# Two groups' value products of batch 0 moved ahead of the first up product, with dummy matmuls behind them

## The chip, the core and the metric

One core of a Trainium2 chip runs the whole program. The metric is the device time of one launch in microseconds (us); below 0.2% of it, a difference can hardly be told from none. Six runs of the kernel before gave 334.09, 333.66, 332.86, 333.53, 332.96 and 333.91 us, median 333.6 us.

## What is computed

The reference is an attention with projected keys and values (8 batches, 8 heads, 1024 positions, head size 64, projected length 64), followed by a two-matrix maximum and an output product:

```python
k_proj = np.einsum('ks,bhsd->bhkd', E, k)
v_proj = np.einsum('ks,bhsd->bhkd', F, v)
scores = scale * np.matmul(q, k_proj.transpose(0, 1, 3, 2))
attn = softmax(scores)                      # over the 64 projected positions
x = attn @ v_proj                           # heads side by side: 8192 x 512
out = np.maximum(x @ w1, x @ w2) @ w_out    # 512 -> 1024 -> 512
```

The kernel takes max(h1, h2) as h2 + relu(h1 - h2): it multiplies x by the weight difference wd = w1 - w2 (the "up product"), applies relu, multiplies by w_out, and adds x @ M with M = w2 @ w_out. Sums are kept in fp32, operands in fp16.

## The kernel before

**Stages.** Each batch goes through an attention part (projections, scores, exponentials, column sums, products with v) and an up and a down part. Batches are cut in two halves of 512 rows (`o` or `j` = 0, 1). From batch 1 on, the up and down parts use a 2x2 block scheme with seven products per unit, whose pieces are interleaved by a list of slots with the attention steps of a later batch. Batch 0 is different: its eight up products per half (`up_slots`, L394) are plain, and beside them the weights are still being prepared: four differences of 256 columns each (`step_wd`, L413, on VectorE), transposes of w2 (`step_w2t`, L419), and the four products that make M (`step_m`, L433, each copied out of PSUM by ScalarE at L440).

**Attention of batch 0.** It is written out by hand in L713 to L747. A group is (g, j): g picks four of the eight heads, j one half of the rows. For each of the four groups there are scores with an exponential on ScalarE (`step_sc`), sums with a logarithm (`step_dn`), the inverse as a second exponential (`step_inv`), and the products with v (`step_at`, L318): 16 small matmuls (`values_into`, L288, tiles of 64x32 with 256 columns, L278) and two multiplications by the inverse sums on VectorE (L325), which write x into `xt_sb`. Half j of x is whole when groups (0, j) and (1, j) have been multiplied; the up product of half j (L400) contracts over four row blocks r, of which r = 0, 1 come from g = 0 and r = 2, 3 from g = 1.

**PSUM banks.** Four banks mm0 to mm3 are handed out in turn by `mm_bank()` (L60, list `turn`, L58); a tile named `att_ps` has two banks and two buffers (`att_banks`, L66). A bank is given to its next writer when its last reader is done. With the last of the products that make M, the slot list reaches key (0, 19): L812 sets `turn` to [2, 3], so that the next bank handed out is mm2, and `step_kv` for batch 1 (its projections of k and v, L172, matmuls at L180) takes it. The first down products, which follow it, name their banks, mm0 and mm1.

**Order.** Every engine runs its instructions in the order in which they are written, under a manual schedule: the order of the list is the order of the queue, and waits are put in by data and buffers. After L747 the slots of L762 follow: the up product 0 of half 0, the value products of group (0, 1), the up product 1 of half 0, those of group (1, 1), the second weight difference, then the up products of half 1 and so on. `warm(n)` (L137) issues n matmuls of 128x512 on a tile of ones, whose result is not used.

**Loads.** k, q, v and the weights come in through GpSimd's DMA queue (L102, L126, L130), in the order of the calls, one after another; the pool for k, v and q has four buffers. Stores and DMA transposes go through SyncE's queue.

```python
    step_at(t, 1, 0)
    step_wd(0)
    ...
    slots = [
        (0, u0[0]), (None, f(step_at, 0, 1)), (1, u0[1]), (None, f(step_at, 1, 1)),
        (None, lambda: loads(1, "v", "q", "k")),
        (None, wd[1]), (2, u1[0]), (3, u1[1]), (4, u0[2]), (None, wt[0]), (5, u0[3]),
```

Of the kernel before, what the change touches and what calls it, by code (L numbers as in the profile page):

```python
# [16 lines left out]
def kernel(  # L17
# [42 lines left out]
    def mm_bank(dtype=FP32, n=None):  # L60
        if n is None:
            n = turn.pop(0)
            turn.append(n)
        return ps.tile([128, 512 if dtype == FP32 else 1024], dtype, tag=f"mm{n}", name="mm_ps")

    def att_banks(dtype=FP32):  # L66
        return ps.tile(
            [128, 2, 512 if dtype == FP32 else 1024], dtype, tag="att", bufs=2, name="att_ps"
        )
# [27 lines left out]
    def load_all(t, b, n, src):  # L97
        alloc(t, n)
        load(t, n, src, b, 0, H)
# [37 lines left out]
    def warm(n):  # L137
        w_ps = mm_bank()
        for _ in range(n):
            nc.tensor.matmul(  # L140
                out=w_ps, lhsT=ones16[:, 0:128], rhs=ones16, start=True, stop=True
            )
# [145 lines left out]
    def values_into(t, g, j, at_ps):  # L288
        for z in range(2):
            tiles_into(  # L290
                lambda o: at_ps[o][:, z * W : (z + 1) * W], t["ex", g, j],
                lambda rows, hh: t["vp"][rows, 4 * g + hh, z, :],
            )

    def new_xt(t):
        t["xt"] = xpool.tile([128, NP2, 2, HALF], FP16, tag="xt", name="xt_sb")

    def x_out(t, g, j):
        return t["xt"][:, 2 * g : 2 * g + 2, :, j * W : (j + 1) * W]
# [15 lines left out]
        ld = t["ld", g, j]  # L315
        nc.scalar.activation(out=ld, in_=ld, func=ACTF.Exp, scale=-1.0)

    def step_at(t, g, j):  # L318
        if "xt" not in t:
            new_xt(t)  # L320
        ld = t.pop(("ld", g, j))
        at_ps = [mm_bank() for _ in range(2)]
        values_into(t, g, j, at_ps)
        for o in range(2):
            nc.vector.tensor_tensor(  # L325
                out=x_out(t, g, j)[:, :, o, :],
                in0=at_ps[o].rearrange("q (z n) -> q z n", z=2),
                in1=ld[:, o, None, :].broadcast_to([128, 2, W]),
                op=ALU.mult,
            )  # L330
# [63 lines left out]
    def up_slots(t, j):  # L394
        t["gt", j] = gt = gpool.tile([128, NFB, HALF], FP16, tag="gt", name="gt_sb")
        for fb in range(NFB):
            def up(fb=fb):
                h_ps = mm_bank()
                for r in range(NDC):
                    nc.tensor.matmul(  # L400
                        out=h_ps,
                        lhsT=wd_sb[:, r, fb * 128 : (fb + 1) * 128],
                        rhs=t["xt"][:, r, :, j * W : (j + 1) * W],
                        start=(r == 0), stop=(r == NDC - 1),
                    )
                if fb < 3:
                    nc.scalar.activation(out=gt[:, fb, :], in_=h_ps, func=ACTF.Relu)
                else:
                    nc.vector.tensor_scalar_max(gt[:, fb, :], h_ps, 0.0)
            yield up  # L410


    def step_wd(f0):  # L413
        nc.vector.tensor_tensor(  # L414
            out=wd_sb[:, :, f0 : f0 + 256], in0=w1_sb[:, :, f0 : f0 + 256],
            in1=w2_sb[:, :, f0 : f0 + 256], op=ALU.subtract,
        )

    def step_w2t(f0):  # L419
        ps_t = mm_bank(FP16)  # L420
        for f in range(2):
            for r in range(NDC):
                nc.tensor.transpose(
                    out=ps_t[:, (f * NDC + r) * 128 : (f * NDC + r + 1) * 128],
                    in_=w2_sb[:, r, f0 + f * 128 : f0 + (f + 1) * 128],
                    identity=ident16,
                )
        fb = f0 // 128
        nc.scalar.copy(
            out=w2t_sb[:, fb : fb + 2, :].rearrange("q f m -> q (f m)"), in_=ps_t  # L430
        )
# [281 lines left out]
    t = tiles[0]  # L713
# [25 lines left out]
    step_dn(t, 1, 0)  # L739
    step_inv(t, 1, 0)  # L740
    step_at(t, 0, 0)
    step_dn(t, 1, 1)
    step_inv(t, 0, 1)
    step_kv(t, 4, 8, "v")
    step_inv(t, 1, 1)
    step_at(t, 1, 0)
    step_wd(0)  # L747


    load_all(tiles[1], 1, "k", k)  # L750
    u0, u1 = [*up_slots(t, 0)], [*up_slots(t, 1)]
    wt = [lambda f0=f0: step_w2t(f0) for f0 in range(0, DF, 256)]
    wd = [lambda f0=f0: step_wd(f0) for f0 in range(0, DF, 256)]
    f = lambda s, *a: lambda: s(tiles[0], *a)

    def loads(b, *names):
        for n in names:
            b_ = b + (n == "k" and b < 2)
            if b_ < B:
                load_all(tiles[b_], b_, n, {"k": k, "v": v, "q": q}[n])  # L760

    slots = [  # L762
        (0, u0[0]), (None, f(step_at, 0, 1)), (1, u0[1]), (None, f(step_at, 1, 1)),
        (None, lambda: loads(1, "v", "q", "k")),
        (None, wd[1]), (2, u1[0]), (3, u1[1]), (4, u0[2]), (None, wt[0]), (5, u0[3]),
        (None, wd[2]), (None, wt[1]), (6, u1[2]), (7, u1[3]), (8, u0[4]), (9, u0[5]), (None, wd[3]),
        (None, wt[2]), (10, u1[4]), (11, u1[5]), (12, u0[6]), (13, u0[7]), (None, wt[3]),
        (14, u1[6]), (15, u1[7]),
# [41 lines left out]
    t = tiles[1]  # L810
    at_slot((0, 19), new_attn, t)
    at_slot((0, 19), lambda: turn.__setitem__(slice(None), [2, 3]))  # L812
    for n, x in enumerate((
# [4 lines left out]
        for name in x.split():  # L818
# [6 lines left out]
            else:  # L825
                g, j = int(name[2]), int(name[3])
# [9 lines left out]
    t = tiles[2]  # L836
# [8 lines left out]
    for b in range(3, B):  # L845
        t = tiles[b]
# [75 lines left out]
```

The softmax here doesn't subtract the row's maximum and nothing guards it: scores larger than these inputs give would overflow.

## Time and profile before

| what | value |
|---|---|
| median of six runs | 333.6 us |
| the profiled execution, its own time | 334.09 us |
| its span (first to last instruction) | 332.3 us |
| TensorE matmul busy | 319.6 us (96%) |
| VectorE busy / ScalarE busy | 239.8 us (72%) / 201.5 us (61%) |
| mean granted TensorE clock | 0.995 |

The profiled execution is also the longest of the six runs. PE is TensorE's matmul, PEld its weight load, DVE is VectorE, ACT ScalarE, POOL GpSimd and SP SyncE. A row of the timeline gives the start, the length, the engine, the line, the operation with its output and inputs, and in brackets how long the engine had been idle and what ended that. A row of the windows gives the length of a stretch, the busy time of each engine in it with the number of instructions in brackets, the granted clock of TensorE as a share of full speed, the DMA share and GB/s. The chain is the work that ended last, followed back step by step; its rows give the start, the length and the work.

### The profile page before, as it was taken

The page shows a single profiled execution, that of the slowest core. Times are in us where ns is not written, and L with a number is a line of the kernel's source. Part 1 is how long each engine was busy: PE and PEld are TensorE (multiplying, and loading weights), DVE is VectorE, ACT ScalarE, POOL GpSimd, SP SyncE. Part 2 cuts the span into 40 slices and gives each one's busy share as a digit, 9 for nine tenths or more (in the row PEclk, how much of TensorE's full clock was granted, in tenths as well). Part 3 has the DMA queues.
Part 4 walks back from the last instruction along what each step waited for, and adds up shares of the span by engine and source line. Part 5 has one row for each costly group of instructions (what it writes and reads, how often), then busy time and mean ns, then how long its engine had stood idle before and what let it go on. Part 6 is the DMA issues. An engine that isn't in the chain of part 4 may idle for free.

```text
span 332.3 us, 9012 instructions
## 1 busy us (share of the span) xinstructions
PE 319.6 (96%) x3852; PEld 247.8 (75%) x3852; DVE 239.8 (72%) x426; ACT 201.5 (61%) x358; POOL 37.1 (11%) x56
## 2 busy tenths in 40 slices
PE   8967999999999999999999999998999999999994
PEld 3532546658888788878887788877887888888883
DVE  1354698988676779677969777776967796969572
ACT  2462522754677677767777677766776777764541
POOL 8546002003000030003000210003000000000000
PEclk9997999999999999999999999999999999999999
DMA  8999999998994969994999699894999321212132
GB/s 150 202 199 197 207 207 192 204 195 150 199 240 126 185 93 224 196 221 85 199 238 200 112 161 242 200 179 67 218 221 190 86 96 34 97 34 95 35 127 96
DMA packets 74681, 53.14 MB, mean 160 GB/s; under 512 B 29457, under 2 KB 74513, under 8 KB 74641
## 3 DMA queue, kind: packets, MB, share of 16 engines
q0 software_dynamic: 29376, 28.31, 53.8%
q1 hardware_dynamic: 45264, 24.25, 30.6%
q8 instruction: 30, 0.49, 0.6%
q14 instruction: 11, 0.08, 0.1%
HBM read 57.15 MB, written 16.78 MB: 222 GB/s over the span
## 4 chain that ended last, share of the span: by engine, by line
PE 85%; DMA 7%; DVE 4%; issue 1%; POOL 1%; ACT 0%; DVEq 0%; SPq 0%; POOLq 0%
PE mm_ps L632 42%; PE mm_ps L554 25%; PE mm_ps L400 4%; PE att_ps L180 3%; DMA big<-in_moe_w_dram 3%; PE mm_ps L266 3%; PE att_ps L278 3%; DMA k_sb<-in_k_dram 2%; PE mm_ps L436 2%; DMA kpt_sb<-kp_sb 1%; DVE xt_sb L325 1%; DVE o_sb L656 1%; PE mm_ps L278 1%; POOL k_sb L102 1%; DVE gt_sb L569 1%
## 5 line engine op out<-in xcount | busy, mean ns | idle before, releaser
L525 ACT COPY p_sb<-mm_ps 128x512 f32<-128x512 f32 x172 | 97.2, 593 | 46.8 <-PE mm_ps L554 33.2
L632 PEld LDWEIGHTS <-big 128*128 128x128 f16 x768 | 73.4, 98 | 12.3 <-issue 3.7
L632 PE MATMUL mm_ps<-T_sb,big 128*128 128x256 f16 x576 | 78.1, 273 | 0.0
L569 DVE TENSOR_TENSOR gt_sb<-mm_ps,p_sb 128x512 f16<-128x512 f32 x56 | 38.5, 688 | 47.6 <-PE mm_ps L554 47.5
L554 PE MATMUL mm_ps<-big,big 128*128 128x256 f16 x336 | 50.4, 273 | 0.0
L554 PEld LDWEIGHTS <-big 128*128 128x128 f16 x448 | 43.8, 98 | 5.2
L632 PEld LDWEIGHTS <-gt_sb 128*128 128x128 f16 x384 | 35.6, 98 | 10.1 <-issue 5.8
L632 PE MATMUL mm_ps<-wo_sb,gt_sb 128*128 128x256 f16 x256 | 42.9, 274 | 0.1
L554 PEld LDWEIGHTS <-wd_sb 128*128 128x128 f16 x336 | 32.9, 98 | 4.1 <-issue 0.3
L554 PE MATMUL mm_ps<-xt_sb,wd_sb 128*128 128x256 f16 x224 | 33.6, 273 | 0.2 <-ACT ex_sb L351 0.2
L351 ACT ACTIVATE ex_sb<-mm_ps 128x512 f16<-128x512 f32 x48 | 26.1, 596 | 10.2 <-PE att_ps L278 7.0
L656 DVE TENSOR_TENSOR o_sb<-mm_ps,p_sb 128x512 f32<-128x512 f32 x32 | 21.9, 684 | 10.7 <-PE mm_ps L632 7.2
L377 DVE TENSOR_TENSOR xt_sb<-att_ps,ld_sb 128x1024 f16<-128x1024 f32 x24 | 29.2, 1218 | 0.1
L632 PE MATMUL mm_ps<-m_sb,xt_sb 128*128 128x256 f16 x128 | 24.4, 273 | 0.0
L604 ACT ACTIVATE gt_sb<-mm_ps 128x512 f16<-128x512 f32 x28 | 16.8, 600 | 8.7 <-PE mm_ps L554 8.7
L515 DVE TENSOR_TENSOR big<-gt_sb 128x1024 f16<-128x1024 f16 x32 | 21.9, 684 | 0.2
L572 DVE TENSOR_SCALAR gt_sb<-gt_sb 128x512 f16<-128x512 f16 (+1 forms) x56 | 20.3, 362 | 1.9
L632 PE MATMUL mm_ps<-wo_sb,big 128*128 128x256 f16 x128 | 21.5, 273 | 0.0
L632 PE MATMUL mm_ps<-T_sb,gt_sb 128*128 128x256 f16 x128 | 21.5, 273 | 0.0
L632 PEld LDWEIGHTS <-xt_sb 128*128 128x128 f16 x192 | 18.8, 98 | 2.2
L229 POOL COPY junk<-kpt_sb 1x1 f16<-1x1 f16 x5 | 0.9, 178 | 167.4 <-DMA kpt_sb<-kp_sb 167.4
L400 PE MATMUL mm_ps<-xt_sb,wd_sb 128*128 128x512 f16 x64 | 16.3, 400 | 3.0 <-DVE wd_sb L414 2.1
(86 smaller groups left out, 434.7 us busy)
## 6 DMA issues: line engine op xcount, KB each, us to landing
out_dram<-o_sb SPq DMA_DIRECT2D x63, 256.0 KB, 2.7
k_sb<-in_k_dram POOLq DMA_DIRECT2D x7, 1024.0 KB, 10.2
v_sb<-in_v_dram POOLq DMA_DIRECT2D x7, 1024.0 KB, 17.2
q_sb<-in_q_dram POOLq DMA_DIRECT2D x7, 1024.0 KB, 22.2
k_sb<-in_k_dram POOLq DMA_DIRECT2D x4, 256.0 KB, 6.6
q_sb<-in_q_dram POOLq DMA_DIRECT2D x4, 256.0 KB, 7.7
v_sb<-in_v_dram POOLq DMA_DIRECT2D x2, 512.0 KB, 12.5
big<-in_moe_w_dram POOLq DMA_DIRECT2D x8, 128.0 KB, 10.6
```

Source lines behind the costliest of these rows:

```text
L278: nc.tensor.matmul(out=dst(r ^ (hh % 2))[hh * Z : (hh + 1) * Z, :], lhsT=weights(rows, hh), rhs=ex[rows, hh % 2, hh // 2 * W : (hh // 2 + ...
L351: nc.scalar.activation(out=t["ex", g, j][:, e, :], in_=banks[e], func=ACTF.Exp, scale=scale)
L377: nc.vector.tensor_tensor(out=x_out(t, g, j).rearrange("q z o n -> q o z n"), in0=at_ps.rearrange("q o (z n) -> q o z n", z=2), in1=ld[:, ...
L400: nc.tensor.matmul(out=h_ps, lhsT=wd_sb[:, r, fb * 128 : (fb + 1) * 128], rhs=t["xt"][:, r, :, j * W : (j + 1) * W], start=(r == 0), stop= ...
L515: nc.vector.tensor_tensor(out=S(i), in0=x, in1=y, op=op)
L525: copy(out=x, in_=bank)
L554: nc.tensor.matmul(out=bank[:, m * W : (m + 1) * W], lhsT=w_[:, n_, (2 * d + m) * 128 : (2 * d + m + 1) * 128], rhs=a[:, n_, :], start=(n ...
L569: nc.vector.tensor_tensor(out=c_blk(j, c), in0=two(x), in1=two(y), op=ALU.add)
L572: nc.vector.tensor_scalar_max(ap, ap, 0.0)
L604: nc.scalar.activation(out=out, in_=in_, func=ACTF.Relu)
L632: nc.tensor.matmul(out=bank[:, i * CH : (i + 1) * CH], lhsT=a(c)[:, i * 128 : (i + 1) * 128], rhs=w_(c), start=(n is not None and m == (lo ...
L656: nc.vector.tensor_tensor(out=o_sb, in0=two(x), in1=two(y), op=ALU.add)
```

## The change

Both remaining value products of batch 0, of groups (0, 1) and (1, 1), are written directly behind `step_wd(0)`, ahead of the first up product, and leave the slot list. They take the two-bank tiles of `att_banks` in place of two banks of the turn each. Four dummy matmuls follow them. The first weight difference, which had stood ahead of the slots already, stands on VectorE ahead of the multiplications of these two groups. In the slot list the loads of the next tiles and the second weight difference change their places relative to the up products of half 1. No instruction of VectorE, ScalarE, GpSimd or SyncE changes its place among those of its own engine: on VectorE the order was already the multiplications of group (1, 0), the first weight difference, those of groups (0, 1) and (1, 1), the second difference. The four multiplications read another PSUM tile. TensorE has the 32 small matmuls at another place and four matmuls with their weight loads more. Between the value products and the end of the preparation `mm_bank()` is called three times less (four banks less for the two groups, one more for the dummies), so that every later bank of the turn in batch 0 is another one than before, up to the reset of `turn` at key (0, 19).

```diff
-    def step_at(t, g, j):
+    def step_at(t, g, j, att=False):
         if "xt" not in t:
             new_xt(t)
         ld = t.pop(("ld", g, j))
-        at_ps = [mm_bank() for _ in range(2)]
+        if att:
+            both = att_banks()
+            at_ps = [both[:, o, :] for o in range(2)]
+        else:
+            at_ps = [mm_bank() for _ in range(2)]
         values_into(t, g, j, at_ps)
...
     step_at(t, 1, 0)
     step_wd(0)
+    step_at(t, 0, 1, True)
+    step_at(t, 1, 1, True)
+    warm(4)
...
     slots = [
-        (0, u0[0]), (None, f(step_at, 0, 1)), (1, u0[1]), (None, f(step_at, 1, 1)),
-        (None, lambda: loads(1, "v", "q", "k")),
-        (None, wd[1]), (2, u1[0]), (3, u1[1]), (4, u0[2]), (None, wt[0]), (5, u0[3]),
+        (0, u0[0]), (1, u0[1]), (None, lambda: loads(1, "v", "q", "k")), (2, u1[0]), (3, u1[1]),
+        (None, wd[1]), (4, u0[2]), (None, wt[0]), (5, u0[3]),
```

## The prediction

> **What bounds the kernel now.** The page first: matmuls fill 319.6 of 332.3 us, and the chain of work that ended last is 85% TensorE. What TensorE loses, the program loses. The row of the 40 slices shows a granted clock below full only in slices 0 and 3; slice 3 (24.9 to 33.2 us) holds the change. So next I read the chain of waits over 20 to 32 us:
>
> ```profile
> 24.58 0.68 DVE xt_sb L325
> 25.25 0.61 DVE wd_sb L414
> 25.86 0.04 issue
> 25.91 1.89 PE mm_ps L400 x4
> 27.80 0.56 PE mm_ps L278 x15
> 28.35 1.25 PE mm_ps L400 x4
> 29.60 0.39 PE mm_ps L278 x16
> ...
> 30.70 0.69 DVE xt_sb L325
> ...
> 31.43 0.59 PE mm_ps L400 x2
> ```
>
> VectorE, TensorE and VectorE take turns here. The value products of groups (0, 1) and (1, 1) (L278 at 27.80 and 29.60) stand behind up products, so their multiplications (L325) end only at 31.38, and the first up product of half 1 goes on at 31.43 with r = 2, 3. The timeline shows who was idle meanwhile:
>
> ```profile
> 23.96 1.29 DVE L325 TENSOR_TENSOR xt_sb<-mm_ps,ld_sb 128x512 f16<-128x512 f32 x2 [0.61 <-ACT ld_sb L316]
> 25.17 0.68 DVE L414 TENSOR_TENSOR wd_sb<-big,big 128x1024 f16<-128x1024 f16 x1
> 25.91 1.89 PE L400 MATMUL mm_ps<-xt_sb,wd_sb 128*128 128x512 f16 x4 [2.09 <-DVE wd_sb L414]
> 28.50 1.29 DVE L325 TENSOR_TENSOR xt_sb<-mm_ps,ld_sb 128x512 f16<-128x512 f32 x2 [2.65 <-ACT gt_sb L407]
> 30.09 1.29 DVE L325 TENSOR_TENSOR xt_sb<-mm_ps,ld_sb 128x512 f16<-128x512 f32 x2 [0.30 <-PE mm_ps L278]
> ```
>
> TensorE waits 2.09 us for the first weight difference; VectorE then has nothing to do for 2.65 us. And 1.89 us for four matmuls is 0.43 us each at first, where 0.216 is the full-speed pitch (16 in 3.45 us at 35.50). The windows say why: the clock is halved for one stretch of 3.41 us, after one in which TensorE was busy for 1.22 us.
>
> ```profile
> 18.67:22.08 3.41, 2.35 (x70) 1.41 (x56) 1.05 (x3) 2.94 (x4) 0.73 (x2) 1.00 1.34 199
> 22.08:25.49 3.41, 1.22 (x32) 0.68 (x26) 2.61 (x6) 1.63 (x3) 3.41 (x5) 1.00 1.44 195
> 25.49:28.90 3.41, 2.99 (x22) 0.86 (x23) 0.76 (x2) 0.60 (x1) 3.41 (x5) 0.50 1.27 203
> ```
>
> **The moved products.** Group (1, 0)'s products start at 23.41. The 32 small matmuls follow at 0.34 to 0.39 us for 16 (chain, 29.60), so they end at about 24.5. Their inputs are there: the two `att_ps` buffers are free after the logarithms (L312), which end at 21.27 and 23.44, and the last inverse ends at 24.47. All of it lies in the 2.09 us wait and costs nothing.
>
> **VectorE.** Its order does not change: the first difference at 25.17 keeps its place, so the first up product still starts at 25.91. The multiplications now follow it directly. A 128x1024 fp16 difference lets the next one start 0.60 us after it (49.00, 49.60, 50.20), and a pair of multiplications takes 1.21 to the next start (23.96 to 25.17). So (0, 1) starts at 25.77 and (1, 1) at 26.98, not 30.09: 3.11 us earlier. It ends at 28.27, and the up product of half 1 goes on at 28.32. The new tile for these reads is costed at nothing: the nearest row, L377 on `att_ps`, does both halves at once in 1218 ns, against 1.29 for the pair; the bounds are -0.15 and +0.1 us in all.
>
> **The dummies.** Four take 4 x 0.216 = 0.87 us, 24.5 to 25.4, inside the wait; without that cover they would cost 0.87. They lift the busy time of the window ending at 25.49 from 1.22 to about 2.7 us (0.7 from the products' move, 0.8 from the dummies) of 3.41, above the 2.35 that kept the full clock. Then eight up matmuls take 1.73 us, 25.91 to 27.64, and r = 0, 1 end at 28.07: TensorE idles 0.25 us, and VectorE sets the 28.32. The Trainium skill speaks otherwise: TensorE: Matmul & The Clock Gate, section "Why this matters for your kernels", asks only that no idle gap exceed about 3 us. By it a gap of 2.09 would not have lowered the clock, and filling it would not be what brings it back; the halved clock would stay, 0.43 us each until 28.9, and r = 2, 3 would start at about 29.55: 1.88 us earlier, not 3.11. I take the row: 1.22 of 3.41 busy, and the clock fell as that stretch ended.
>
> **The shifted banks.** Counted from the top, the dummies take mm2, which before was the first up product's. Behind them come 16 up products, 4 transposes and 4 products of M, 24 calls in all, so that the last of these (L436) is in mm2 again; before, four more calls (the groups') stood among them, the first up product was the first of 28, and the last was in mm1. The projections of batch 1 (L180), next on TensorE, ask for mm2, because the turn is reset there. Before, mm2 held the first product of M, long copied, and mm1's next writer came over 1.85 us later. The edge, before:
>
> ```profile
> 51.87 0.40 PE L180 MATMUL mm_ps<-k_sb,eft 128*64 128x512 f16 x1
> ...
> 51.97 0.59 ACT L440 CAST m_sb<-mm_ps 128x512 f16<-128x512 f32 x1 [1.14 <-PE mm_ps L436]
> ```
>
> The projections must now wait for that copy: 51.97 + 0.59 + 0.04 for the release is 52.60, against 51.87: 0.73 us of bare TensorE idling (bounds 0.6 and 0.8). Queued behind it is every later matmul; the chain from 51.94 to 66.69 has no slack, so it is lost in full. ScalarE and VectorE idle there anyway (1.29 and 1.04 us before their next copies).
>
> **Fixed dates.** Loads do not move: GpSimd's order is unchanged, and up to the load issued at 54.08, which a projection releases, nothing on its queue waits for shifted work. Issue plus landing against the new need: last weights 24.92 + 7.7 = 32.6, where the third difference is due at 32.59 and its matmul 0.8 us behind the difference's end; w_out 37.7 against 41.5; v of batch 1 at 48.1 against 49.5; its q at 28.26 + 25.1 = 53.36, needed at 56.06 - 3.11 + 0.73 = 53.68. That one is close: 2.65 us earlier is the most it allows. q of batch 2 lands at 70.65 either way, and its transposes are in by 78.5 (GpSimd's gate), against scores at 82.56 - 2.38 = 80.2. The later loads are released by work that shifts too.
>
> **The sum.** 3.11 - 0.73 = 2.38 us: span 332.3 - 2.4 = 329.9, time 334.09 - 2.38 = 331.7. That execution was the longest of six. The halved clock depends on where the stretch of 3.41 us falls, which may differ by run: with full clock before, its first two up products and the products between would have ended 1.5 us sooner, near 332.6; the runs lie between. The changed kernel should miss that spread and lie near 331.7, 1.9 us (0.6%) under the median of 333.6.
>
> **Rivals.**
> - *The bank wait costs nothing* (the copy is hidden, or I counted the turn wrongly): then 3.11 is cut to 2.65 by q of batch 1: 331.4. Against it: the named banks and the contiguous chain. 0.14.
> - *The clock still falls at 25.5*, as small 64x32 matmuls and four dummies might not count enough: 1.88 - 0.73 = 1.15, 332.9. For it: the skill's rule, and that nothing in the trace shows the threshold between 36% and 69% busy. Against: the estimated 79%. 0.12.
> - *Slower: the clock stays halved through two stretches*, 25.5 to 32.3. Then TensorE, bound by its matmuls from 25.9 on, loses half of 6.4 us less the 0.25 slack, 2.95: 331.7 + 2.95 = 334.6. It decides only if the stretch from 25.49 is judged idle too; before, one that was 2.99 of 3.41 busy restored the clock. 0.03.
> - *A load is later than in this trace*: each 0.1 us of q of batch 1 past 53.7 costs 0.1; by 1 us, 332.4. Inside the range. 0.08.
>
> The likeliest, 331.7 within 0.4, has 0.63. The range, 331.0 to 332.9, takes in the bounds of the copy and the multiplications (0.3 together), the first rival, the late load, and the upper rival's time. Below 0.2% (0.67 us, about what a measurement of this kernel tells from no change), that is below 332.9, lie the main case, the first and last rival and part of the second: faster 0.88; same 0.08; slower 0.04.
>
> **What would show it.** The first up product's four matmuls at 25.9 in about 0.9 us, clock 1.00 in every stretch; multiplications of L329 at 25.8 and 27.0; the second up product of half 0 without products between; the first matmuls of L180 for batch 1 near 49.5 with a wait of about 0.7 us for ScalarE's copy (L444); no wait for q of batch 1. A clock of 0.50 after 25.5 means the second rival; no gap ahead of L180 the first. I am wrong if a wait that I called hidden appears between 28 and 70 us.

## The result, and the profile after

The changed kernel takes 331.29 us in the median of 18 runs (330.07 to 332.64), the kernel before 333.58 us in 39 runs taken beside it and earlier. The ratio is 0.9932, with a 95% interval of 0.9917 to 0.9947: 2.3 us faster (1.8 to 2.8). Forecast were 331.7 us: a difference of 2.38 us within one execution, and of 1.9 us against the median of 333.6.

The profiled execution has a span of 328.3 us, 4.0 less than the one of before, which is more than the 2.3 us by which the medians differ. To see what of it belongs to the change, I cut each profiled execution at three points that all kernels here have: the start of the first weight difference on VectorE, the end of the first 20 matmuls of the up products (five products, half 1 begun), and the first matmul of batch 1's projections (L180). What lies before the first point is the start-up, which no kernel here changes. (From L329 on, lines of the changed kernel stand four further down: its L404 is L400 of before.)

| kernel | start-up | to the 20th up matmul | to L180 of batch 1 | rest | span |
|---|---|---|---|---|---|
| before | 25.17 | 8.58 | 18.12 | 280.46 | 332.3 |
| changed | 24.48 | 5.45 | 18.86 | 279.51 | 328.3 |

The change is in the middle columns: 3.13 us less and 0.74 us more. The other 1.6 us are the start-up, 0.69, where v landed earlier, and the rest, 0.9, which has one place, shown further down. The prediction spoke of neither.

The slices of the page after have no dip in the clock any more:

```profile
PEclk9999999999999999999999999999999999999999
```

The timeline of the changed kernel around the first up product, the rows that answer to those of before:

```profile
22.95 0.62 PE L278 MATMUL att_ps<-ex_sb,vp_sb 64*32 64x256 f16 x32
23.28 1.29 DVE L329 TENSOR_TENSOR xt_sb<-mm_ps,ld_sb 128x512 f16<-128x512 f32 x2 [0.61 <-ACT ld_sb L316]
23.50 1.04 PE L140 MATMUL mm_ps<-ones 128*128 128x512 f16 x4
24.48 0.68 DVE L418 TENSOR_TENSOR wd_sb<-big,big 128x1024 f16<-128x1024 f16 x1
25.08 2.48 DVE L329 TENSOR_TENSOR xt_sb<-att_ps,ld_sb 128x512 f16<-128x512 f32 x4
25.22 4.71 PE L404 MATMUL mm_ps<-xt_sb,wd_sb 128*128 128x512 f16 x20 [0.68 <-DVE wd_sb L418]
```

Both value products (32 small matmuls) and the dummies fit into the wait, of which 0.68 us is left; the four multiplications follow the weight difference without a gap; and 20 up matmuls run in one row of 4.71 us. The chain shows who sets the pace now, VectorE with a bare 0.04 us between:

```profile
26.36 1.21 DVE xt_sb L329 x2
27.57 0.04 issue
27.61 2.32 PE mm_ps L404 x10
```

The windows, at the same times as before (busy times in the order PE, PEld, DVE, ACT, POOL, then clock, DMA share, GB/s), have the full clock in both:

```profile
22.08:25.49 3.41, 2.21 (x58) 1.03 (x55) 2.64 (x5) 1.63 (x3) 3.41 (x6) 1.00 1.43 195
25.49:28.90 3.41, 3.35 (x16) 1.42 (x15) 2.67 (x5) 1.79 (x3) 3.38 (x5) 1.00 1.24 199
```

And the chain at the end of M's products has the new wait:

```profile
41.86 6.27 PE mm_ps L440 x29
48.13 0.02 issue
48.16 0.59 ACT m_sb L444
48.75 0.04 issue
48.79 1.92 PE mm_ps L180 x16
```

Before, L180 followed L436 directly. Now ScalarE's copy lies between them on the path.

### The profile page after: what moved, and what is told of

Its sections match the earlier page's. It is cut to its first block, busy times and chain, and to the rows that moved or that the text cites. A ratio compares the mean times of both kernels' runs of the same rounds, so it can differ in the third digit from the quotient of the medians.

```text
span 328.3 us, 9020 instructions
## 1 busy us (share of the span) xinstructions
PE 318.6 (97%) x3856; PEld 248.6 (76%) x3856; DVE 239.8 (73%) x426; ACT 201.4 (61%) x358; POOL 36.9 (11%) x56
## 4 chain that ended last, share of the span: by engine, by line
PE 86%; DMA 5%; DVE 3%; POOL 2%; issue 1%; ACT 1%; DVEq 0%; POOLq 0%
PE mm_ps L636 43%; PE mm_ps L558 25%; DMA v_sb<-in_v_dram 4%; PE mm_ps L404 4%; PE att_ps L180 3%; PE att_ps L278 3%; PE mm_ps L266 3%; PE mm_ps L440 2%; DMA big<-in_moe_w_dram 2%; DVE xt_sb L329 1%; POOL q_sb L102 1%; DVE o_sb L660 1%; POOL k_sb L102 1%; DVE gt_sb L573 1%; PE mm_ps L180 1%
## 5 line engine op out<-in xcount | busy, mean ns | idle before, releaser
L573 DVE TENSOR_TENSOR gt_sb<-p_sb 128x512 f16<-128x512 f32 x28 | 19.1, 681 | 0.0
```

Of the source, the lines that this page charges most:

```text
L573: nc.vector.tensor_tensor(out=c_blk(j, c), in0=two(x), in1=two(y), op=ALU.add)
```

## The experiments

My theory: the 3.13 us have two parts, the clock and the order, and 0.74 us of them are given back by a bank that the shifted turn makes late. The rivals: the clock's fall has another cause than the idle time, so the dummies do nothing; and the bank wait is hidden, or is taken back by something later, so that it costs no time. Each run below is compared with the kernel before beside it. The table of stretches at the end puts them side by side.

**The bank wait taken away.** The dummies name their bank, and the turn runs as before:

```diff
-    def warm(n):
-        w_ps = mm_bank()
+    def warm(n, bank=None):
+        w_ps = mm_bank(n=bank)
...
-    warm(4)
+    warm(4, 2)
```

> The changed kernel with the dummies in bank mm2 by name, so that the turn of the banks runs as before and the projections of batch 1 find mm2 long copied. Theory (the shifted turn costs 0.7 us): the wait of 0.67 us ahead of L180 for ScalarE's copy is gone, and the time lies 2.7 to 3.1 us under the kernel before (2.65 is what q of batch 1 allowed in the first profile, 3.1 if its load is sooner), against 2.3 for the changed kernel. Rival (that wait is hidden later): 2.3 us under, as the changed kernel.

Measured: 331.42 us in 6 runs, ratio 0.9934 (0.9914 to 0.9955). The wait is gone from the chain, L180 follows L440 at once, and the stretch is 18.12 us again:

```profile
44.18 6.91 PE mm_ps L440 x32
51.09 1.85 PE mm_ps L180 x16
```

The time did not show it: 2.1 us under the kernel before, where 2.7 to 3.1 were expected. The wait costs its 0.74 us in the stretch, which is what the theory says of it; whether it costs time stayed open after six runs and was taken up again below.

**The bank wait put into the kernel before.** The turn is moved on by one, nothing else:

```diff
     step_at(t, 1, 0)
     step_wd(0)
+    turn.append(turn.pop(0))
```

> The kernel before with the turn of the banks moved on by one ahead of the first up product, nothing else: the last product of M then falls into mm2, which the projections of batch 1 ask for. Theory: a wait of about 0.7 us for ScalarE's copy ahead of L180, and 0.7 us over the kernel before. Rival (hidden behind work that follows): no difference.

Measured: 333.94 us in 22 runs, ratio 1.0017 (1.0002 to 1.0031): 0.6 us slower (0.1 to 1.0), for 0.74 us in the stretch (18.86 against 18.12). The same chain rows appear in it, with ScalarE's copy between:

```profile
53.57 0.59 ACT m_sb L440
...
54.20 1.92 PE mm_ps L180 x16
```

So three calls of `mm_bank()` less, or one more, has a price some 20 us later. What follows L180 is as long as before (280.42 against 280.46 us), so in this execution nothing hides the wait, and the rival of a hidden wait falls for this kernel. Its cost in time is less sure than 0.6 us: five of the 22 runs have a mean granted clock of 0.99 or less, against two of the 33 beside them, and among the runs at 0.991 to 0.996 (14 and 28) the difference of the means is 0.4 us (resampled 95% interval 0.1 to 0.7).

**Dummies alone.** The kernel before with four dummies behind the first weight difference, in mm2 by name:

```diff
     step_at(t, 1, 0)
     step_wd(0)
+    warm(4, 2)
```

> The kernel before with four dummies in mm2 by name behind the first weight difference, nothing else. They lift the stretch from 1.22 to about 2.1 of 3.41 us. Theory (the busy share of the stretch sets the clock): clock 1.00 at 26 to 29 us, the first up product in 0.9 us, and the time 1.0 to 1.5 us under the kernel before. Rival (an idle gap under 3 us does not matter, the fall has another cause): clock 0.50 as before, no difference. What is then left to the changed kernel with the bank kept, 1.3 to 2 us, is the products' move.

Measured: 332.26 us in 12 runs, ratio 0.9961 (0.9949 to 0.9974): 1.3 us faster, and 1.35 us in the stretch (7.23 against 8.58). The timeline has the four dummies, and the up product behind them in 1.04 us where it took 1.89, although the rest of the idling is still there:

```profile
24.00 1.04 PE L140 MATMUL mm_ps<-ones 128*128 128x512 f16 x4
...
26.15 1.04 PE L400 MATMUL mm_ps<-xt_sb,wd_sb 128*128 128x512 f16 x4 [1.12 <-DVE wd_sb L414]
```

One profile could be luck of the moment, but the mean granted clock of each run is on record too. One stretch of 3.41 us at half clock takes 0.005 off the mean over 332 us, and a mean of 0.995 or less was granted in 0 of these 12 runs, and in 30 of the 33 of the kernel before beside them. Dummies do set the clock here. The move of the products, on top of them, is worth the other 1.78 us of the 3.13.

**No dummies.** The changed kernel without them (the turn is then as before):

```diff
     step_at(t, 1, 1, True)
-    warm(4)
```

> The changed kernel without its four dummies; the turn then also gives the projections of batch 1 a free bank. TensorE's busy time in the stretch ahead of the first up product is about 1.9 of 3.41 us. Theory A (the dummies are what holds the clock): the clock falls to 0.50 behind that stretch, the second stretch of up products takes 0.43 us a matmul, and the time lies about 1.9 us under the kernel before, 1.1 above the one with dummies and the bank kept. Theory B (the products' move alone is enough, or only a long gap counts): clock 1.00, and the time is that of the kernel with dummies and the bank kept, 2.7 to 3.1 us under.

> No dummies, once more. If the clock never falls without them: the stretches are 3.13 and 20.51 us and the time is that of the kernel with the bank kept. If it falls in some executions, by where the stretch of 3.41 us lies: the profile shows a clock of 0.50 behind 26 us and a first stretch of 4.2 to 4.5 us, or single runs lie 1.2 us above the others.

Measured: 331.23 us in 6 runs, ratio 0.9927 (0.9907 to 0.9946), and again 331.89 us in 22 runs, ratio 0.9944 (0.9927 to 0.996). The two profiles are of one program and differ in the clock. First the timeline row of the first execution, then of the second:

```profile
26.80 4.71 PE L404 MATMUL mm_ps<-xt_sb,wd_sb 128*128 128x512 f16 x20 [1.65 <-DVE wd_sb L418]
```

```profile
25.96 6.18 PE L404 MATMUL mm_ps<-xt_sb,wd_sb 128*128 128x512 f16 x20 [1.65 <-DVE wd_sb L418]
```

The wait ahead is 1.65 us in both. In the second, the clock falls at 26.39 and comes back at 29.80, 3.41 us later; its windows, cut at these times:

```profile
22.98:26.39 3.41, 1.28 (x50) 0.78 (x51) 2.80 (x6) 1.63 (x3) 3.41 (x5) 1.00 1.42 197
26.39:29.80 3.41, 3.41 (x9) 1.22 (x8) 2.50 (x5) 1.19 (x2) 3.19 (x5) 0.50 1.23 189
```

Where do the edges of the stretches lie in the first? The falls within one trace are whole steps of 3.413 us apart: in the execution with the turn shifted they begin at 8.00, 28.48 and 332.26 us, which are 6 and 89 steps. In the first execution without dummies the clock falls only at 328.35 us, when TensorE is done. Counted back by 89 and 90 steps from there, the stretches around the wait are these:

```profile
21.15:24.56 3.41, 2.40 (x80) 1.53 (x83) 2.04 (x4) 2.50 (x5) 2.63 (x4) 1.00 1.44 193
24.56:27.97 3.41, 1.76 (x54) 0.89 (x31) 3.11 (x6) 1.18 (x4) 3.41 (x5) 1.00 1.32 202
```

The edge falls before the products here, so that up products lie in the same stretch as the wait: 1.76 us busy, and the clock holds. In the second execution the edge falls at the end of the wait: 1.28 us busy, and the clock falls. So neither theory of the first expectation holds by itself: without dummies the clock falls in some executions and not in others, by where the stretch's edge lies. A fall costs 1.47 us (6.92 against 5.45): the move of the products alone is worth all 3.13 us in the one execution and 1.66 in the other. With four dummies behind the moved products it fell there in none of eight profiles.

The times of single runs spread too widely to show two groups, but their clocks do: 0.995 or less in 99 of 110 runs of the kernel before, 11 of 28 without dummies, and 6 of 51 of the changed kernel. Where in the program a run's clock fell is known from the profiles alone, and some falls lie in the start-up. In the time, what the dummies are worth in the changed kernel, the bank wait that they bring included, is not shown: over all runs the means are 331.60 us without them (28 runs) and 331.33 with them (51), 0.3 us apart with a resampled 95% interval of 0.1 the other way to 0.65.

**No dummies, and the banks of the turn.** The moved products written as before, into two banks of the turn each:

```diff
-    step_at(t, 0, 1, True)
-    step_at(t, 1, 1, True)
-    warm(4)
+    step_at(t, 0, 1)
+    step_at(t, 1, 1)
```

> No dummies, and the moved products in four banks of the turn, as they were written before, in place of the two-bank tiles. Group (1, 1)'s products then wait for the multiplications of group (1, 0), and the first up product, in mm2, for the first multiplication of group (0, 1), some 0.6 us later than with the two-bank tiles; TensorE idles longer ahead of it. Theory: at full clock the first stretch is 3.5 us, 0.4 more than with the two-bank tiles and no dummies; if the clock falls, 5 to 5.6 us. The second stretch is 20.51 us. Rival (the two-bank tiles are not needed): 3.13 us.

Measured: 332.7 us in 14 runs, ratio 0.998 (0.9961 to 0.9999). The products of group (1, 1) wait for group (1, 0)'s multiplications (0.33 us), and the first up product for the first of group (0, 1) (0.79 us), so that it starts 1.34 us behind the difference's start, not 0.74. The clock fell here too:

```profile
24.95 0.41 PE L278 MATMUL mm_ps<-ex_sb,vp_sb 64*32 64x256 f16 x15 [0.33 <-DVE xt_sb L329]
...
26.15 6.16 PE L404 MATMUL mm_ps<-xt_sb,wd_sb 128*128 128x512 f16 x20 [0.79 <-DVE xt_sb L329]
```

The stretch is 7.50 us, 0.58 above the execution without dummies in which the clock fell: that is what the two-bank tiles spare where the clock falls. They may also spare some of the falls: a mean clock of 0.995 or less was granted in 11 of these 14 runs, and in 11 of 28 with the two-bank tiles.

**Does the bank wait cost time in the changed kernel?** The changed kernel and the one with the bank kept, three more times each, side by side. (The expectations cut at the start of the matmuls r = 2, 3 of half 1, ten matmuls earlier than the tables here; the 3.13 us in them is the length of that first part, which was 6.26 before.)

> The changed kernel once more, so that it runs beside the two variants on one chip. By the stretches of the profile: from the first weight difference to the matmuls r = 2, 3 of half 1 3.13 us (6.26 before), from there to the projections of batch 1 21.18 us (20.51 before, the bank wait of 0.67 us). Time 2.3 us under the kernel before.

> The dummies in mm2 by name, once more. By the stretches: 3.13 and 20.51 us, so 0.67 us less than the changed kernel, of which q of batch 1 gives back about 0.1 to 0.4 where the loads are late. Time 2.7 to 3.0 us under the kernel before, 0.3 to 0.7 under the changed kernel beside it. Rival: no difference from the changed kernel, because the loads of batch 1 and 2 take it back.

> The changed kernel, for more executions beside the kernel with the bank kept, whose time does not show the 0.7 us that its second stretch does. Theory A (the late fourth transpose of batch 6, 0.9 us, falls by chance on either): it is late in some profile of the changed kernel too, and over all runs the bank kept is 0.3 to 0.7 us faster. Theory B (without the bank wait something later takes the time back): it is never late here and mostly late there, and the times stay equal within 0.2 us.

> The bank kept, beside the run before it on the same chip. Second stretch 20.44 against 21.18 us in any case. Theory A: 0.3 to 0.7 us under the changed kernel over all runs. Theory B: equal within 0.2 us, with the fourth small transpose landing after 4.2 us instead of 2.7, or a wait of the batch 1 transposes for q.

> The changed kernel once more, for the same comparison: stretches 3.13 and 21.18 us; whether the fourth small transpose is late.

> The bank kept once more, for the same comparison: stretches 3.13 and 20.44 us; whether the fourth small transpose is late, and whether q of batch 1 is waited for.

Measured, changed kernel: 331.54 us in 18 runs (ratio 0.9939, 0.9918 to 0.996), 331.37 in 7 (0.9932, 0.9907 to 0.9956), 331.6 in 8 (0.9925, 0.99 to 0.995). Bank kept: 331.31 in 22 runs (0.9945, 0.9928 to 0.9961), 331.4 in 6 (0.9925, 0.9896 to 0.9954), 330.11 in 6 (0.9893, 0.9865 to 0.992). Over all runs, the means are 331.33 us (51 runs) and 331.22 us (40 runs): 0.1 us less with the bank kept, with a resampled 95% interval of 0.5 less to 0.25 more. The gain expected there was not found: a gain of up to 0.45 us can't be excluded, but the full 0.74 us can.

The profiles show where part of it goes. With the bank kept, TensorE reaches loads that no kernel here moves sooner. In the third execution, the third weight difference and then the transposes of batch 1's q waited for them:

```profile
33.25 0.69 DVE L418 TENSOR_TENSOR wd_sb<-big,big 128x1024 f16<-128x1024 f16 x1 [0.91 <-DMA big<-in_moe_w_dram]
34.00 0.39 PE L404 MATMUL mm_ps<-xt_sb,wd_sb 128*128 128x512 f16 x1 [0.22 <-DVE wd_sb L418]
...
53.43 0.73 PE L237 MATMUL mm_ps<-ident,q_sb 128*128 128x128 f16 x10 [0.16 <-DMA q_sb<-in_q_dram]
```

In the first, q alone (TensorE's weight load waited 0.3 us for it); in the fourth, neither, and that is the shortest span of all, 327.8 us. In the second, the fourth of the small DMA transposes of `kp_sb` (batch 6) was late: 4.4 us from issue to landing, where the others take 2.7, and TensorE waited 1.1 us. So neither of the two theories came out as written: the transpose was never late in the changed kernel, and late in one of four with the bank kept. From the last two stretches together, the changed kernel needs 298.4 us in each of its four profiles; with the bank kept it is 297.8, 298.7, 298.3 and 297.6, on average 0.3 less, in keeping with the runs. In part the load dates take the 0.74 us back, and in one execution of four the late transpose did; how much of it is left in the time is not resolved.

That late transpose is also the 0.9 us by which the profiles of before and after differ in the rest. The chain of the kernel before:

```profile
222.04 4.22 DMA kpt_sb<-kp_sb
226.26 0.04 issue
226.31 0.41 PE mm_ps L266 x16
```

| kernel | start-up | to the 20th up matmul | to L180 | rest | late transpose |
|---|---|---|---|---|---|
| before | 25.17 | 8.58 | 18.12 | 280.46 | yes |
| turn shifted | 26.83 | 8.51 | 18.86 | 280.42 | yes |
| dummies only | 25.41 | 7.23 | 18.12 | 280.46 | yes |
| no dummies, first | 26.07 | 5.44 | 18.12 | 280.47 | yes |
| no dummies, again | 25.22 | 6.92 | 18.11 | 280.46 | yes |
| banks of the turn | 24.81 | 7.50 | 18.12 | 280.53 | yes |
| changed, second to fourth | 25.97, 24.76, 24.64 | 5.45 each | 18.86 each | 279.51 each | no |
| bank kept, first | 27.45 | 5.45 | 18.12 | 279.64 | no |
| bank kept, second | 26.86 | 5.45 | 18.12 | 280.60 | yes |
| bank kept, third | 24.85 | 5.45 | 18.51 | 279.77 | no |
| bank kept, fourth | 24.74 | 5.45 | 18.12 | 279.53 | no |

It is late in one of eight profiles of kernels with moved products and dummies, and in all six of the others; one program has it both ways. It is the same transpose each time and not the same moment (it is issued between 219.8 and 224.4 us where it is late). What makes it late was not found. Seven late ones spread by chance over fourteen profiles would fall so unevenly about once in 400 times, so the counts alone speak for a link with the change. The times speak against a firm one: with the transpose always late before and never after, the difference would be 3.13 - 0.74 + 0.9 = 3.3 us, and the runs show 2.3 (1.8 to 2.8). It stays open.

## Why the prediction was right, step by step

- **The moved products and VectorE's order**: 3.11 us were worked out, 3.13 measured. The multiplications start 0.60 us behind the difference and end 3.08 us behind its start, as the row of other differences said; the two-bank tile costs nothing.
- **The dummies**: right that they and the products keep the clock, though in one execution in two the products alone did. The clock of 1.00 also bears out the row of the trace against the Trainium skill's table (TensorE: Matmul & The Clock Gate, "Why this matters for your kernels"), which asks only that no gap exceed about 3 us: a gap of 1.65 us was followed by a fall in one execution. The same page's Part 1 (the section on the HAM clock gate) has the windows free-running, and that fits the two executions without dummies. For this wait the busy time of the stretch that holds it sorts all fourteen profiles, each cut at its own edges, counted from its own falls: the clock fell behind 1.22, 1.28, 1.31 and 1.62 of 3.41 us (before, no dummies again, turn shifted, banks of the turn), and held at 1.76 (no dummies, first), 1.89 (dummies only) and 2.07 or more (the eight with moved products and dummies). It is no rule for the whole program: in the start-up the clock fell behind stretches with 1.83, 1.93 and 2.40 us busy, and what counts there was not found. My estimate of 2.7 for the changed kernel was too high, for the window cut at the old times (2.21) and for its own stretch (2.31), without harm.
- **The shifted banks**: 0.73 us worked out, 0.74 measured, in the place named. "Lost in full" agrees with the kernel before (0.6 us, within 0.1 to 1.0) and not with the changed one: with the bank kept at most 0.45 us came back. The rival by which the wait costs nothing was wrong about the wait, which is there in all four profiles, and nearer about the time than its 0.14.
- **Fixed dates**: q of batch 1 was called close, and the last weights were put at 32.6 us against a need at 32.59. These are the two that TensorE waited for, once the bank wait was gone. In the changed kernel TensorE waited for neither; the third difference on VectorE waited for the weights in two of its four profiles (0.38 and 0.16 us), off the path.
- **The sum**: 2.38 us against 2.3 measured (1.8 to 2.8). Set against the profiled execution it gave 331.7, and the runs gave 331.29; the term that was off is the 0.5 us between that execution and the median. I put it down to the clock, and forecast that the runs of the changed kernel would lie closer together. They span 2.6 us. A run of the kernel before that escapes the fall is indeed faster (332.0 us in the mean at a clock of 0.997 or more, against 333.7), but only 11 of 110 do. More of the spread is the start-up: the first weight difference starts anywhere from 24.48 to 27.45 us in fourteen profiles, whatever the kernel. So the mechanism, 3.11 - 0.73 against 3.13 - 0.74 in the stretches, is what was shown; that two medians with such a spread differ by 2.3 us and not by 1.9 or 2.7 is no further proof of it.
- **Rivals**: the clock's fall stayed away with the dummies in this place, and the slower case with it. The late load did not come to hold TensorE up in the changed kernel's four profiles.

## What to carry to other kernels

When TensorE waits and another engine stands idle behind work that TensorE could do in that wait, move that work into it; what the move is worth is read from the row of the idle engine, here VectorE. Where buffers are handed out in turn, count the turn to its next fixed point after any edit: three calls less put a 0.6 us copy on the path some 20 us later, though not all of it showed in the time. And cut several profiles at common points before a difference of two spans is believed: here 1.6 of 4.0 us were start-up and a late transfer.

## What the runs showed of the hardware

- One program, the same wait of 1.65 us, and the clock halved for 3.41 us in one execution and not in the other: the stretch of 3.41 us that held the wait was busy for 1.28 us in the one and 1.76 in the other. In all nine profiles with four dummies in the wait the clock held there; a fall costs 1.5 us.
- The clock can fall in the start-up as well: with the bank kept, first execution, it was 0.58 from 9 to 12 us. In the three profiles with such a fall the first weight difference came at 26.83 to 27.45 us, in the eleven others at 24.48 to 26.07.
- A small DMA transpose that lands after 2.7 us in most cases took 4.2 to 4.4 us in seven of fourteen profiles, always the fourth of five, with nearly no transfers on the engines by the time it landed.
